# FFN gate/up pieces in four batches of eight instead of eight batches of four, with the down pieces regrouped between them

## The chip, the cores and the metric

One core of one Trainium2 chip. The time is the device time of one execution in microseconds (us); three runs of the kernel before gave 257.48, 257.58 and 261.14, so the median is 257.58 us. A profile is one further execution, recorded instruction by instruction.

## The reference, cut to what matters

```
g   = sigmoid((x * gate_w).sum(-1))                  # a gate per token, 2048 tokens of 1024
q, k, v = split(x @ wqkv); pq, pk = phi(q), phi(k)   # phi: x+1 above 0, else exp(x), plus 1e-6
kv  = sum over tokens of pk^T v, z = sum of pk       # linear attention, 32 heads of 32
a   = (pq kv / (pq z + 1e-6)) @ wo
i   = argmax(x @ w_r);  s = x[i]                     # ONE token goes through the FFN
y   = ((silu(s @ w_gate) * (s @ w_up)) @ w_down) * sigmoid((x @ w_r)[i])
b   = x, with y added to row i
out = g * a + (1 - g) * b
```

w_gate and w_up are 1024 x 3584, w_down is 3584 x 1024, all bf16. One token uses them, so in the FFN there is little to compute and 22 MB of weights to fetch.

## The kernel before, in words

TensorE is fed in units. A K/V unit (`unit_KV(t, nb)`) is eight matmuls of 128x512 for the 128 tokens of block t and a quarter nb of the K and V columns; a Q unit (`unit_Q`) is eight such matmuls for the queries; `unit_KVACC(t)` is eight short matmuls that add block t to the kv sums. ScalarE and VectorE turn each unit's PSUM tile into phi (`phi_exp`, `phi_evac`) and free it; there are four such tiles. The main loop (L510 to L530) runs over t = 4 to 15: four K/V units, the KVACC of the block before after the second of them, then one or two Q units.

The FFN of the chosen token is hung into this loop in pieces. A gate/up piece (`gate_up`) is one load of 128 rows of w_gate or w_up (L385; 512 KB in the first half of the columns, 384 KB in the second) and four matmuls that use 32 columns of the array each, side by side. Eight pieces add up in one PSUM tile; after the eighth piece of gate comes silu (exp on ScalarE; add, reciprocal and product on VectorE), after the eighth of up the product h. A half is therefore 16 pieces, first gate, then up. `h_transpose` (called by `ffn_flush` at the next FFN step) turns h into columns. A down piece (`down_rows`) is one load of two groups of 128 rows of w_down (L433, 512 KB) and two VectorE operations on 128x1024 (L441, L443) that add into `yacc`. There are 14: the first eight need the first half of h only.

All pieces share one ring of nine SBUF tiles (`ffw`, FFN_DEPTH = 9). `ffn_pieces` (L447) gives the order in which they are fetched and used. `ffn_prefetch` (L458) keeps nine in flight: a load goes to the queue of SP as soon as a piece has been used, and its tile must have been released. The first nine loads stand behind the fetch of the chosen row (L358); after the last piece comes a copy of x to the scratch tensor xp (L464), into which the finished row is written later (L504).

GU_AFTER (L34) says after which unit a batch of gate/up pieces is used: (7, 1) is after the K/V unit (7, 1), (7, "end") after the Q units of t = 7. DOWN_STEPS (L35) gives the VectorE steps of the down pieces, from t = 9 on. From the router on, `strict[0]` is False: the wrapper of L77 then writes no program order for TensorE, VectorE and ScalarE, and the framework's scheduler orders each engine's instructions at compile time, by its own idea of when operands are there and which instruction stands earlier in the program. In the trace TensorE's order is the program's nearly everywhere. [...]

Of the kernel before, what the change touches and what calls it, by code (L numbers as in the profile page):

```python
# [30 lines left out]
LN1EPS = math.log1p(EPS)  # L31
N_WARM = 6
Q_PER_T = {4: 2, 5: 1, 6: 1, 7: 2, 8: 1, 9: 1, 10: 2, 11: 1, 12: 1, 13: 2, 14: 1, 15: 0}
GU_AFTER = {(6, "end"), (7, 1), (7, "end"), (8, 1), (8, "end"), (9, "end"), (10, "end"), (11, "end")}  # L34
DOWN_STEPS = {9: (1, 1, 1, 1), 10: (1, 1, 1, 1), 11: (1, 1, 1, 1), 12: (1, 1, 1, 1, 1), 13: (1, 1, 1, 1), 14: (1, 1, 1, 1), 15: (1, 1, 1)}  # L35
FFN_DEPTH = 9
NORM_PER_T = [2, 0, 0, 3, 3, 3, 3, 3, 3, 3, 3, 3, 3, 3, 3, 3]
# [3 lines left out]
def kernel(  # L41
# [180 lines left out]
    def unit_KV(t, nb):  # L222
        kv_open(t)
        ps = ps_work.tile([P, 512], F32, tag="w")
        kv_mm(ps, t, nb, 0, KC)
        kv_evac(ps, t, nb)

    def unit_KVACC(t):
        for g in range(NG):
            pe.matmul(kv_slot(g), lhsT=pk_t[t][:, g * P : (g + 1) * P], rhs=vt_t[t][:, g, :],  # L230
                             start=False, stop=False, skip_group_check=True)
        del pk_t[t], vt_t[t]

    def unit_Q(g, j):
        ps = ps_work.tile([P, 512], F32, tag="w")
        for c in range(KC):
            pe.matmul(ps[:], lhsT=wq[:, c, g * P : (g + 1) * P], rhs=xT[:, c, 512 * j : 512 * j + 512],
                             start=(c == 0), stop=(c == KC - 1))
        phi_evac(ps[:], pq_all[:, g, 512 * j : 512 * j + 512])
# [104 lines left out]
    def router_part1():  # L344
        strict[0] = True
        dve.tensor_reduce(out=rmax[:], in_=c4[:, :, 0], axis=mybir.AxisListType.X, op=ALU.max)
        pen = rt.tile([1, 4], F32)
        strict[0] = False
        dve.tensor_scalar(pen[:], c4[:, :, 0], rmax[0:1, 0:1], None, op0=ALU.is_equal)
        dve.tensor_scalar(pen[:], pen[:], -1.0e6, 1.0e6, op0=ALU.mult, op1=ALU.add)  # L350
        dve.tensor_tensor(pen[:], pen[:], c4[:, :, 1], op=ALU.add)
        idx_f = rt.tile([1, 1], F32)
        dve.tensor_reduce(out=idx_f[:], in_=pen[:], axis=mybir.AxisListType.X, op=ALU.min)
        idx_i = rt.tile([1, 1], I32)
        dve.tensor_copy(idx_i[:], idx_f[:])
        nonlocal_idx[0] = idx_val = nc.values_load(idx_i[0:1, 0:1], engines=(mybir.EngineType.Pool,), min_val=0, max_val=S - 1)
        nc.gpsimd.dma_start(out=xsel_row[:], in_=x2d[bass.ds(idx_val, 1), :])
        xsel_ld[0] = nc.gpsimd.dma_start(out=xsel4[0:128:32, :], in_=x2d[bass.ds(idx_val, 1), :].rearrange("o (j n) -> (o j) n", j=4))  # L358
        dve.tensor_copy(rmax_bf[:], rmax[:])

    def router_part2():
        xs_ps = ps_ffn.tile([P, KC + 1], F32, tag="f")
        for c in range(KC):
            pe.matmul(xs_ps[:, c : c + 1], lhsT=xsel_row[0:1, c * P : (c + 1) * P], rhs=one_bf[0:1, 0:1],
                             start=True, stop=True)
        pe.matmul(xs_ps[:, KC : KC + 1], lhsT=ones_row[0:1, :], rhs=rmax_bf[0:1, 0:1], start=True, stop=True)
        dve.tensor_copy(xs_pad[:, :, 0], xs_ps[:, 0:KC])
        act.activation(sig[:], xs_ps[:, KC : KC + 1], ACTF.Exp, scale=-1.0)
        dve.tensor_scalar_add(sig[:], sig[:], 1.0)
        dve.reciprocal(sig[:], sig[:])  # L370
# [55 lines left out]
    def down_rows():  # L426
        wdv = B_w_down.rearrange("(k p) n -> p k n", p=P)
        pairs = [(7 * j + b, 1) for b in (0, 2) for j in range(4)]
        pairs += [(7 * j + 4, 1) for j in range(4)] + [(6, 7), (20, 7)]
        for i2, (k0, dk) in enumerate(pairs):  # L430
            def load(k0=k0, dk=dk):
                wt = ffw.tile([P, 2048], BF, tag="ffw")
                ld = nc.sync.dma_start(out=wt[:].rearrange("p (k n) -> p k n", k=2), in_=wdv[:, k0 : k0 + dk + 1 : dk, :])  # L433
                tc.add_manual_dep(ld.ins, ffn_state["last_ld"].ins.name, NOSYNC, reason="queue order")
                ffn_state["last_ld"] = ld
                return wt

            def compute(wt, kk, i2=i2, k0=k0, dk=dk):
                w, h1 = wt[:, 1024 * kk : 1024 * kk + 1024], hcol[:, k0 + dk * kk : k0 + dk * kk + 1]
                if i2 == 0 and kk == 0:  # L440
                    dve.tensor_scalar(yacc[:], w, h1, None, op0=ALU.mult)  # L441
                else:
                    dve.scalar_tensor_tensor(yacc[:], w, h1, yacc[:], op0=ALU.mult, op1=ALU.add)  # L443

            yield load, compute

    def ffn_pieces():  # L447
        gu, dn = gate_up(1), down_rows()
        yield from gate_up(0)
        for _ in range(4):  # L450
            yield from islice(gu, 4)
            yield from islice(dn, 2)
        yield from dn

    pieces = ffn_pieces()
    inflight = deque()

    def ffn_prefetch():  # L458
        while len(inflight) < FFN_DEPTH:
            nxt = next(pieces, None)  # L460
            if nxt is None:
                if not ffn_state.get("copied"):
                    ffn_state["copied"] = True
                    cp = nc.sync.dma_start(out=xp[:], in_=x2d)  # L464
                    tc.add_manual_dep(cp.ins, ffn_state["last_ld"].ins.name, NOSYNC, reason="queue order")
                    ffn_state["last_ld"] = cp
                    gate_logits()
                return
            inflight.append((nxt[0](), nxt[1]))

    def ffn_flush():
        pend = ffn_state.pop("pending", None)
        if pend is not None:
            pend()

    def ffn_step(n):
        for _ in range(n):
            ffn_flush()
            wt, comp = inflight.popleft()
            comp(wt)  # L480
            ffn_prefetch()
# [3 lines left out]
    def down_step(n):  # L485
        for _ in range(n):
            ffn_flush()
            if down["cur"] is None:
                down["cur"] = inflight.popleft()
            wt, comp = down["cur"]  # L490
            comp(wt, down["n"] % 2)
            if down["n"] % 2:
                down["cur"] = None
                ffn_prefetch()
            down["n"] += 1
# [14 lines left out]
    for t in range(4, NT):  # L510
        for nb in range(4):
            unit_KV(t, nb)
            if nb == 1 and t > 4:
                unit_KVACC(t - 1)
            if (t, nb) in GU_AFTER:
                ffn_step(4)
            steps = DOWN_STEPS.get(t, ())
            if nb < len(steps):
                down_step(steps[nb])
        for i in range(Q_PER_T[t]):  # L520
            unit_Q(*q_units.popleft())
            if 4 + i < len(steps):
                down_step(steps[4 + i])
            if t == 4 and i == 0:
                router_part1()
                ffn_prefetch()
        if t == 5:
            router_part2()
        if (t, "end") in GU_AFTER:
            ffn_step(4)  # L530
    unit_Q(*q_units.popleft())
    unit_KVACC(NT - 1)
    down_finish()
# [4 lines left out]
    for i in range(3):  # L538
        n = 3 if i < 2 else 2
# [3 lines left out]
    for i in range(3):  # L543
        n = 3 if i < 2 else 2
# [135 lines left out]
```

## Time and profile before

| what | value |
|---|---|
| median of three runs | 257.58 us |
| the profiled execution: its time | 257.94 us |
| its span, first to last instruction | 256.4 us |
| mean granted TensorE clock | 0.998 |
| TensorE busy | 249.9 us, 97% of the span |
| VectorE, ScalarE, GpSimd busy | 145.7, 126.9, 47.0 us |
| matmuls of a gate/up batch, first half / second half | 16 in 1.05 us / 16 in 0.83 us |
| one step into `yacc` | 1281 ns, 27 of them, and a first of 753 ns |
| first weight load issued; copy to xp issued | 57.44 us; 125.62 us |

A line of a timeline gives start, duration, engine, line, operation, tile written <- tiles read, and count. Nearly all compute instructions carry L77, because a wrapper there records them; they are told apart by their tiles: `ps<-wkv,xT` is K/V, `ps<-xT,wq` is Q, `ps<-wt,xs_pad` is gate/up, `yacc<-wt` is down. The engine SPq with `wt<-in_B_w_gate_dram` and its like is the issue of a weight load; the data lands later, and "to landing" says how much later.

### The profile page before, as it was taken

How to read it: one execution, taken by the hardware profiler on the slowest of the kernel's cores; microseconds unless marked ns; L12 is line 12 of the kernel's file. 1: busy time of each engine (PE TensorE's matmuls, PEld its weight loads, DVE VectorE, ACT ScalarE, POOL GpSimd, SP SyncE). 2: the span in 40 equal slices, each digit the busy share in tenths (PEclk: the TensorE clock that was granted, in tenths of full speed). 3: DMA queues.
4: the chain of work that ended last, by engine and by line, in shares of the span. 5: the costliest groups of instructions: out<-in, count | busy, mean ns of one | idle time of the engine just before them, and what ended most of it. 6: DMA issues, size and time to landing. Idle time of an engine off the chain costs nothing.

```text
span 256.4 us, 3781 instructions
## 1 busy us (share of the span) xinstructions
PE 249.9 (97%) x1400; PEld 116.6 (45%) x1426; DVE 145.7 (57%) x238; ACT 126.9 (49%) x202; POOL 47.0 (18%) x99
## 2 busy tenths in 40 slices
PE   8999999999999999999999999999999999999994
PEld 3444454454444444444444444444444444444443
DVE  0055024324155368996899723575986779954443
ACT  2195324545354444654445646466899732352210
POOL 6000001010000000000000000012997029960000
PEclk9999999999999999999999999999999999999999
DMA  6999992007999999879898100077000473454222
GB/s 189 307 330 189 238 315 76 0 3 239 354 348 348 340 336 344 255 227 328 270 438 276 4 0 0 4 234 237 1 3 0 121 233 119 164 179 149 84 82 82
DMA packets 47257, 47.71 MB, mean 186 GB/s; under 512 B 18364, under 2 KB 35140, under 8 KB 47176
## 3 DMA queue, kind: packets, MB, share of 16 engines
q1 hardware_dynamic: 46952, 47.34, 60.3%
q8 instruction: 11, 0.18, 0.3%
q0 software_dynamic: 256, 0.14, 0.2%
q14 instruction: 6, 0.05, 0.1%
q10 hardware_dynamic: 32, 0.00, 0.0%
HBM read 39.34 MB, written 8.40 MB: 186 GB/s over the span
## 4 chain that ended last, share of the span: by engine, by line
PE 95%; DMA 2%; issue 1%; SPq 1%; DVE 0%
PE ps L77 87%; PE kvacc L77 3%; PE first L77 2%; DMA wkv<-in_A_wqkv_dram 2%; PE dps L77 1%; PE rps L77 1%; SPq L77 1%; PE yps L77 0%; DVE ot L77 0%; PE pt L77 0%; PE xs_ps L77 0%; PE hps L77 0%; PE wps L77 0%
## 5 line engine op out<-in xcount | busy, mean ns | idle before, releaser
L77 PE MATMUL ps<-wkv,xT 128*128 128x512 bf16 x467 | 107.2, 380 | 0.6
L77 PEld LDWEIGHTS <-xT 128*128 128x128 bf16 x512 | 48.7, 98 | 58.9 <-issue 4.2
L77 PE MATMUL ps<-xT,wq 128*128 128x512 bf16 x249 | 58.0, 380 | 0.3
L77 ACT ACTIVATE u<-ps 128x512 f32<-128x512 f32 x60 | 35.8, 596 | 40.5 <-PE ps L77 37.2
L77 PE MATMUL ps<-m_sb,pq_all 128*128 128x512 bf16 (+1 forms) x259 | 55.2, 373 | 0.4 <-issue 0.2
L77 ACT ACTIVATE e<-u 128x512 f32<-128x512 f32 x64 | 40.4, 632 | 1.7
L77 PEld LDWEIGHTS <-pq_all 128*128 128x128 bf16 x264 | 25.7, 98 | 29.9 <-issue 0.4
L77 PEld LDWEIGHTS <-wq 128*128 128x128 bf16 x256 | 24.8, 98 | 30.4 <-issue 0.8
L594 POOL TENSOR_TENSOR pq_all<-pq_all,rb 128x512 bf16<-128x512 bf16 x32 | 36.0, 1160 | 8.7 <-DVE rb L77 8.7
L77 DVE SCALAR_TENSOR_TENSOR yacc<-wt,hcol,yacc 128x1024 f32<-128x1024 bf16 x27 | 34.6, 1281 | 3.7 <-DMA wt<-in_B_w_down_dram 3.1
L77 ACT CAST vt<-ps 128x512 bf16<-128x512 f32 x32 | 18.8, 588 | 34.5 <-PE ps L77 34.5
L77 DVE SCALAR_TENSOR_TENSOR pq_all<-ps,e 128x512 bf16<-128x512 f32 x32 | 21.6, 684 | 21.3 <-ACT e L77 21.3
L77 DVE SCALAR_TENSOR_TENSOR ot<-ps,gate,xg 128x512 bf16<-128x512 f32 (+1 forms) x33 | 23.7, 725 | 16.5 <-PE ps L77 15.0
L77 ACT ACTIVATE xg<-xt,omg 128x1024 f32<-128x1024 bf16 x16 | 18.2, 1147 | 25.9 <-DVE ot L77 25.9
L77 DVE SCALAR_TENSOR_TENSOR pk<-ps,e 128x512 bf16<-128x512 f32 x28 | 19.2, 687 | 20.1 <-ACT e L77 20.1
L77 DVE STREAM_SHUFFLE rb<-rdp 128x512 f32<-128x512 f32 x32 | 22.4, 736 | 0.0
L209 POOL MEMSET vt<- 128x8 bf16 x16 | 1.9, 137 | 105.7 <-PE kvacc L77 105.7
L77 PEld LDWEIGHTS <-pk 128*128 128x128 bf16 x128 | 8.5, 98 | 3.3 <-issue 0.4
L77 PE MATMUL kvacc<-vt,pk 128*128 128x129 bf16 x128 | 9.7, 221 | 0.1
L77 ACT CAST m_sb<-ps 128x512 bf16<-128x512 f32 x16 | 9.3, 583 | 0.0
L77 PE MATMUL first<-wkv,xT 128*128 128x512 bf16 x31 | 7.8, 396 | 0.6 <-DMA wkv<-in_A_wqkv_dram 0.6
L77 DVE RECIPROCAL rd<-dn 128x512 f32<-128x512 f32 x2 | 6.7, 3353 | 2.1 <-ACT dn L77 2.1
(96 smaller groups left out, 76.4 us busy)
## 6 DMA issues: line engine op xcount, KB each, us to landing
wt<-in_B_w_down_dram SPq DMA_DIRECT2D x14, 512.0 KB, 5.7
wt<-in_B_w_gate_dram SPq DMA_DIRECT2D x8, 512.0 KB, 7.0
wt<-in_B_w_up_dram SPq DMA_DIRECT2D x8, 512.0 KB, 8.8
xt<-xp SPq DMA_DIRECT2D x16, 256.0 KB, 2.7
out_dram<-ot SPq DMA_DIRECT2D x15, 256.0 KB, 2.0
wt<-in_B_w_gate_dram SPq DMA_DIRECT2D x8, 384.0 KB, 7.6
wt<-in_B_w_up_dram SPq DMA_DIRECT2D x8, 384.0 KB, 7.1
wkv<-in_A_wqkv_dram SPq DMA_DIRECT2D x8, 256.0 KB, 5.0
```

What stands on the lines that cost most here:

```text
L77: inst = fn(*a, **k)
L209: nc.gpsimd.memset(vt_t[t][:, :, 128:129], 1.0)
L594: nc.gpsimd.tensor_tensor(sl, sl, rb[:], op=ALU.mult)
```

## The change

Three things are edited. Half of the places in GU_AFTER go, and at each of the four that stay eight pieces are used instead of four: a whole gate or up accumulation of one half. The first place stays (6, "end"), so pieces 5 to 8 are used there and no longer at (7, 1). And the order of the second half's pieces changes: before, it was four gate/up, two down, four times over; now it is two down, eight gate, four down, eight up, and the other eight down. FFN_DEPTH, DOWN_STEPS and all the rest stay.

```diff
-GU_AFTER = {(6, "end"), (7, 1), (7, "end"), (8, 1), (8, "end"), (9, "end"), (10, "end"), (11, "end")}
+GU_AFTER = {(6, "end"), (8, 1), (9, "end"), (11, "end")}
...
         yield from gate_up(0)
-        for _ in range(4):
-            yield from islice(gu, 4)
-            yield from islice(dn, 2)
+        for n in (2, 4):
+            yield from islice(dn, n)
+            yield from islice(gu, 8)
         yield from dn
...
             if (t, nb) in GU_AFTER:
-                ffn_step(4)
+                ffn_step(8)
...
         if (t, "end") in GU_AFTER:
-            ffn_step(4)
+            ffn_step(8)
```

## The prediction

> **What bounds the kernel now.** I read, in this order: the page (busy times, chain of waits), the timeline of TensorE around the gate/up batches, the timeline of SP with the landings of the loads, and the stages as windows. From the page:
>
> ```profile
> PE 249.9 (97%) x1400; PEld 116.6 (45%) x1426; DVE 145.7 (57%) x238; ACT 126.9 (49%) x202; POOL 47.0 (18%) x99
> ...
> PE 95%; DMA 2%; issue 1%; SPq 1%; DVE 0%
> ```
>
> TensorE carries 95% of the chain that ended last. From the first weight load to the end it is never idle for more than 0.2 us, so a microsecond that is added to its stream, as work or as waiting, is a microsecond of the kernel; and one saved is saved. TensorE's timeline at the first two batches:
>
> ```profile
> 65.80 1.89 PE L77 MATMUL ps<-xT,wq 128*128 128x512 bf16 x8
> 67.62 1.05 PE L77 MATMUL ps<-wt,xs_pad 128*32 128x512 bf16 x16
> 68.60 3.63 PE L77 MATMUL ps<-wkv,xT 128*128 128x512 bf16 x15
> 72.06 0.64 PE L77 MATMUL kvacc<-vt,pk 128*128 128x129 bf16 x8
> 72.63 1.17 PE L77 MATMUL ps<-wt,xs_pad 128*32 128x512 bf16 x16
> ```
>
> The batch at 67.62 takes 1.05 us, its twin at 72.63 takes 1.17: the second already waited about 0.1 us for a load. Which one? SP's timeline, then the answers on the tile wt for the issues at 60.8 and 62.1 and for the one at 65.95, then the stages as windows (length, busy time of PE, PEld, DVE, ACT, POOL, granted clock, DMA share, GB/s):
>
> ```profile
> 57.44 8.47 SPq L385 DMA_DIRECT2D wt<-in_B_w_gate_dram  x8
> 65.95 1.41 SPq L385 DMA_DIRECT2D wt<-in_B_w_up_dram  x1
> ```
>
> ```profile
> L385 SPq DMA_DIRECT2D wt<-in_B_w_gate_dram x2: 1170/1843/2516, 60.8 to 62.1; - x2
> ...
> DMA to landing us min/median/max: 9.8/9.8/9.8
> ```
>
> ```profile
> L385 SPq DMA_DIRECT2D wt<-in_B_w_up_dram x1: 1410/1410/1410, 66.0 to 66.0; - x1
> ...
> DMA to landing us min/median/max: 8.9/8.9/8.9
> ```
>
> ```profile
> 69.10:73.40 4.30, 4.30 (x36) 2.09 (x36) 1.30 (x2) 2.33 (x4) 0.13 (x1) 1.00 1.09 348
> ```
>
> The seventh gate load lands at 62.05 + 9.8 = 71.85, the ninth load of all (up) at 65.95 + 8.9 = 74.86. The loads are one stream of 512 KB at 348 GB/s, 1.5 us each, so the eighth gate load, between the two, lands at about 73.35. That is when the batch at 72.63 could finish: its last piece starts at 73.39. The pieces are used about as fast as they arrive. Counting back by 1.5 us: the fourth piece landed at 67.3, the fifth lands at 68.85, the sixth at 70.35.
>
> [...] Matmuls of 512 columns start 0.2155 us apart within a kind; from the last Q matmul (67.311) to the first gate/up one (67.620) it is 0.309, from the last gate/up group (68.278) to the next K/V matmul (68.599) it is 0.321, and the one after it comes 0.01 late: 0.093 + 0.105 + 0.01 = 0.21 us per batch. In the second half (384 columns) it is 0.309 and 0.267 - 0.163, the same. [...]
>
> **The change, part by part.**
>
> 1. Four batches fewer. The matmuls are the same 128; four switches in and out go: 4 x 0.21 = -0.84 us. The 0.1 us wait of the batch at 72.63 goes as a place of its own: -0.10.
>
> 2. The first batch wants eight loads where four are there. It stays at 67.62. With eight pieces its last group would start at 67.62 + 7 x 0.2155 = 69.13, but its load lands at 73.35, so it starts at about 73.39 as before. [...] behind the waiting matmul are the K/V units of t = 7, which hid this wait before (4.0 us, 68.60 to 72.63). Cost: 73.39 - 69.13 = +4.26 us. The stall comes in pieces of about 1.3 us, a group of matmuls whenever a load lands. ScalarE, VectorE and their PSUM tiles only run dry; nothing of theirs is late afterwards beyond what TensorE is.
>
> 3. Does the stream of loads catch up later? Nothing can be won back: TensorE has no other wait in this stretch that the delay could fill. Nor does the next batch wait. Pieces 1 to 4 free their tiles as before, 5 to 8 sooner, so the stream runs on at its rate, piece 16 lands near 85.4, and batch two comes near 88.4 (73.72 where K/V resumes, plus the 15.06 us of units between, less two switches of 0.2).
>
> 4. The new order of the loads. Ten loads (the second down piece on) now wait for batch two instead of following single pieces. The queue runs empty from about 87 to 89. Each later batch has one piece that depends on a down piece:
>  - The eighth gate piece of the second half takes the tile of the first down piece, so it is issued after two yacc steps. Those follow h_transpose, which follows K/V (9, 0): from the end of batch two 4 x 1.73 + 0.3 + 0.3 + (0.75 + 0.68 + 1.28) = 10.2 us, plus 3.3 to 3.5 us to land on an empty queue (a down load issued at 114.86 took 3.5): 13.7. Batch three wants this piece after eight units, a KVACC and the transpose, 14.7, and seven pieces of 0.163, so 15.8: margin 2.1 us.
>  - The eighth up piece takes the tile of the fifth down piece: two loads of slack less, but six units later; margin about 4 us.
>  - 16 yacc steps are left after batch four: 16 x 1.285 + 8 phis of 0.68 = 26 us from about 128, ending near 154.5; the sum over yacc is wanted at 163.3 + 3.3: margin 12.
>  - The copy to xp, last on SP's queue: eight down loads from 127 (12 us) and the copy's own 12 us (129.9 to 141.93 before) end near 151.5; row and gates need it at about 167. GpSimd's queue is moved past nothing: its row write waits for VectorE's brow as before.
>  I cost part 4 at nothing; if the first margin were used up, each microsecond past it would be one on TensorE.
>
> Sum against the profiled execution: 257.94 + 4.26 - 0.84 - 0.10 = 261.26. The median of the runs lies 0.36 below that execution, so I give 260.9 us, +1.3%. A measurement of this kernel tells about 2% (5.15 us) from no change.
>
> **The unknown in it: the order that the scheduler chooses.** Program order is not forced here, and the scheduler does move a batch behind K/V work when it thinks its operands late: at 92.02 two K/V matmuls stand before the batch of (8, "end"), whose PSUM tile was not yet free. If it thinks the loads late at (6, "end"), it puts K/V matmuls of t = 7 between the pieces. Two things speak against that. Batch (7, 1) stands in program order although its last load was late on the chip. And in these lines of VectorE and of ScalarE
>
> ```profile
> 118.47 1.28 DVE L77 SCALAR_TENSOR_TENSOR yacc<-wt,hcol,yacc 128x1024 f32<-128x1024 bf16 x1 [2.45 <-DMA wt<-in_B_w_down_dram]
> 119.67 0.68 DVE L77 SCALAR_TENSOR_TENSOR pk<-ps,e 128x512 bf16<-128x512 f32 x1
> ```
>
> ```profile
> 117.11 0.63 ACT L77 ACTIVATE e<-u 128x512 f32<-128x512 f32 x1
> ```
>
> a yacc step stands ahead of a phi that was ready at 117.74 and comes earlier in the program; the step's load landed at 118.37. So the scheduler had it landing at least 0.6 us sooner than it did: it is an optimist about loads. From both sides: all of the wait filled, -0.94 us; none, +3.32. I take none.
>
> **Rivals.**
>
> - A, as above: the pieces in program order, the clock stays. 260.9 us. Chance 0.58.
> - B, half filled: the scheduler sees the last pieces 1 to 2 us late and puts five to nine K/V matmuls ahead of them. Each 0.2155 us moved up saves that, each extra switch costs 0.2: the gain is about 1.4, 259.5 us. Chance 0.16.
> - C, the other side, not slower: its idea of the loads is as slow as the chip's, and the K/V units (6, "end") to (7, 1) fill the wait wholly. Then only the switches count: 257.58 - 0.94 = 256.6, or up to 257.6 with pieces split. It decides if the eighth load is expected about 4 us after the last Q matmul; from 3.3 us of filling on there is no loss. For it: the matmuls exist and depend on nothing. Against: the optimism shown. Chance 0.07.
> - D, the clock: for 5 us TensorE works 15% of the time. [...] Against: no gap is over 1.4 us. From 1.8 us on it makes the kernel over 2% slower. Chance 0.12.
> - E, a second stall: the margin of 2.1 us in part 4 fails, or VectorE stands behind a down load so long that the four PSUM tiles fill. For it: VectorE did stand 2.45 us at 118.47. Against: four tiles are some 5 us of units. 1 to 3 us more: 262 to 264. Chance 0.07.
>
> **The numbers.** Predicted is A, 260.9. The range 258.3 to 263.5 holds A, B, the lower halves of D and E; left out are C and the tails, about 0.15. Over 2% faster (under 252.4) no case reaches: 0.01. Over 2% slower (over 262.7): most of D and about half of E, 0.12. The rest, 0.87, is within 2%, nearly all of it on the slow side.
>
> **What would show it.** Right: one line of gate/up matmuls at about 67.6 that lasts some 6 us, with waits for DMA wt inside; K/V resuming near 73.7; four batches near 67.6, 88.4, 104.9 and 126; after that TensorE as dense as before and shifted by 3.3. Clock 1.00 in the window from 73 to 80 excludes D. K/V matmuls between gate/up ones near 68 to 73 show B or C. A wait on w_gate near 105 shows E. If K/V resumes near 69.4, the loads were earlier than I think and the reading of the landings is wrong.

## The result, and the profile after

The kernel after takes 265.76 us (median of four runs, 264.72 to 267.13), the kernel before 257.54 (four runs): ratio 1.029 over all runs, 95% interval 1.021 to 1.038 (the two medians alone give 1.032). It is slower, in the forecast direction, but by two and a half times what was forecast (+8.2 us instead of +3.3) and above the range's end of 263.5. The profiled execution took 265.26 us with a span of 263.7, 7.3 more than before; mean clock 0.986 instead of 0.998.

The page of the kernel after, its first section, TensorE's clock in 40 slices and the chain that ended last:

```profile
PE 251.4 (95%) x1400; PEld 117.4 (45%) x1426; DVE 145.3 (55%) x238; ACT 126.9 (48%) x202; POOL 47.0 (18%) x99
...
PEclk9999999999959999999999999999999999999999
...
PE 84%; DMA 8%; SPq 3%; DVE 3%; issue 1%; ACT 0%; DVEq 0%; POOLq 0%
```

TensorE's part of the chain fell from 95% to 84%; loads, the queue that issues them and VectorE now stand in it. And in one slice (72 to 79 us) the clock was granted at about half. TensorE's timeline there:

```profile
67.89 1.05 PE L77 MATMUL ps<-wt,xs_pad 128*32 128x512 bf16 x16
69.20 0.40 PE L77 MATMUL ps<-wt,xs_pad 128*32 128x512 bf16 x4 [0.27 <-DMA wt<-in_B_w_gate_dram]
70.70 0.40 PE L77 MATMUL ps<-wt,xs_pad 128*32 128x512 bf16 x4 [1.10 <-DMA wt<-in_B_w_gate_dram]
72.21 0.62 PE L77 MATMUL ps<-wt,xs_pad 128*32 128x512 bf16 x4 [1.10 <-DMA wt<-in_B_w_gate_dram]
73.72 0.62 PE L77 MATMUL ps<-wt,xs_pad 128*32 128x512 bf16 x4 [0.90 <-DMA wt<-in_B_w_gate_dram]
74.27 0.61 PE L77 MATMUL ps<-wkv,xT 128*128 128x512 bf16 x1
75.10 5.06 PE L77 MATMUL ps<-wkv,xT 128*128 128x512 bf16 x14 [0.22 <-issue]
80.00 0.64 PE L77 MATMUL kvacc<-vt,pk 128*128 128x129 bf16 x8
```

Pieces 5 to 8 come one by one, 1.5 us apart, each when its load lands. The K/V matmuls of t = 7, which need no FFN weight, stand behind them and start only at 74.27: TensorE kept its order through the whole wait. The records then get longer, 0.62 instead of 0.40 for the same four matmuls. The stages as windows (length, busy PE, PEld, DVE, ACT, POOL, granted clock, DMA share, GB/s):

```profile
68.65:72.06 3.41, 1.09 (x16) 0.20 (x8) 0.69 (x1) 0.60 (x1) 0.00 (x0) 1.00 1.09 348
72.06:78.89 6.83, 5.57 (x18) 1.86 (x19) 3.78 (x2) 1.55 (x3) 0.00 (x0) 0.50 1.09 348
78.89:82.30 3.41, 3.41 (x23) 1.84 (x22) 1.98 (x3) 1.50 (x3) 0.13 (x1) 1.00 1.09 347
```

After 3.41 us with TensorE busy for 1.09 of them the clock is 0.50, for 6.83 us, two such windows. Later there is one more wait, shown by TensorE's timeline, by the chain of waits around it and by VectorE's timeline:

```profile
130.60 1.90 PE L77 MATMUL ps<-wkv,xT 128*128 128x512 bf16 x8
133.56 0.23 PE L77 MATMUL hps<-sel,h_bf 128*128 128x4 bf16 x3 [1.06 <-DVE h_bf L77]
```

```profile
125.00 1.20 DVE yacc L77
...
126.22 3.51 DMA wt<-in_B_w_down_dram
...
129.83 1.30 DVE yacc L77
...
131.15 1.28 DVE yacc L77
132.43 0.60 DVE pq_all L77
133.03 0.48 DVE h_bf L77
...
133.56 0.23 PE hps L77 x3
```

```profile
129.83 2.61 DVE L77 SCALAR_TENSOR_TENSOR yacc<-wt,hcol,yacc 128x1024 f32<-128x1024 bf16 x2 [3.03 <-DMA wt<-in_B_w_down_dram]
132.35 0.68 DVE L77 SCALAR_TENSOR_TENSOR pq_all<-ps,e 128x512 bf16<-128x512 f32 x1
132.95 0.55 DVE L77 TENSOR_TENSOR h_bf<-ps,sg 128x384 bf16<-128x384 f32 x1
```

The last step of the sixth down piece (125.00) frees a ring tile; only then is the seventh down load issued (126.22), which takes 3.51 us to land. VectorE has two of that piece's steps ahead of the product h of the second half and stands idle 3.03 us until the load lands; the transpose of h on TensorE (`hps`) waits for h. In the program it is the other way round: by the end of t = 11 only twelve steps into `yacc` have been written, then comes h, then the seventh piece. In the trace fourteen stand ahead of h (sixteen in before): the scheduler moved two of them forward.

The sum, from the two traces. The last group of the first batch starts 73.72 - 67.89 = 5.83 us after the first instead of 7 x 0.2155 = 1.51: +4.32. From there to the KVACC it is 6.28 us, at full clock 16 x 0.2155 + 0.33 = 3.78: +2.50. From K/V (12, 0) to the next KVACC it is 4.77 us, before 3.54: +1.23. Four switches and the old small wait, as priced in the prediction: -0.94. Together +7.1, and the first batch began 0.27 us later: +7.4, measured +7.3.

### The profile page after: what moved, and what is told of

Same layout as the page of the kernel before. It is cut to its first block, busy times and chain, and to the rows that moved or that the text cites. A ratio compares the mean times of both kernels' runs of the same rounds, so it can differ in the third digit from the quotient of the medians.

```text
span 263.7 us, 3784 instructions
## 1 busy us (share of the span) xinstructions
PE 251.4 (95%) x1400; PEld 117.4 (45%) x1426; DVE 145.3 (55%) x238; ACT 126.9 (48%) x202; POOL 47.0 (18%) x99
## 4 chain that ended last, share of the span: by engine, by line
PE 84%; DMA 8%; SPq 3%; DVE 3%; issue 1%; ACT 0%; DVEq 0%; POOLq 0%
PE ps L77 77%; DMA wt<-in_B_w_gate_dram 3%; SPq L385 3%; PE kvacc L77 3%; PE first L77 2%; DMA wkv<-in_A_wqkv_dram 2%; DVE yacc L77 2%; DMA wt<-in_B_w_down_dram 1%; DMA xsel<-in_A_x_dram 1%; PE dps L77 1%; PE rps L77 1%; SPq L77 1%; DVE pq_all L77 0%; ACT u L77 0%; DVE pk L77 0%
## 5 line engine op out<-in xcount | busy, mean ns | idle before, releaser
L77 PE MATMUL ps<-wkv,xT 128*128 128x512 bf16 x467 | 109.4, 384 | 0.9 <-issue 0.2
L77 PEld LDWEIGHTS <-xT 128*128 128x128 bf16 x512 | 49.5, 99 | 60.7 <-issue 6.3
L77 DVE SCALAR_TENSOR_TENSOR pk<-ps,e 128x512 bf16<-128x512 f32 x28 | 19.2, 687 | 15.8 <-ACT e L77 15.8
L77 PE MATMUL ps<-wt,xs_pad 128*32 128x512 bf16 (+1 forms) x128 | 8.0, 368 | 3.4 <-DMA wt<-in_B_w_gate_dram 3.4
```

The costliest lines, as they stand in the source:

```text
L77: inst = fn(*a, **k)
```

## The experiments

The theory had these three terms: the wait for loads, the clock after it, and the second wait. Rivals: the clock falls for another reason; the second wait is only a consequence of the delay; VectorE simply has too much to do there. Ratios are against the kernel before on the same chip (its median was 257.9 to 258.4).

**One part alone: the first batch.** The kernel before, with its order of the pieces; only the first two batches are joined.

```diff
-GU_AFTER = {(6, "end"), (7, 1), (7, "end"), (8, 1), (8, "end"), (9, "end"), (10, "end"), (11, "end")}
+GU_AFTER = {(6, "end"): 8, (7, "end"): 4, (8, 1): 4, (8, "end"): 4, (9, "end"): 4, (10, "end"): 4, (11, "end"): 4}
...
-                ffn_step(4)
+                ffn_step(GU_AFTER[(t, nb)])
...
-            ffn_step(4)
+            ffn_step(GU_AFTER[(t, "end")])
```

> Before with one part of the change alone: the first two batches (pieces 1 to 8) are used together after (6, end); all other batches of four and the old order of the pieces stay. Three-term theory (4.3 us of waiting for loads 5 to 8, then 2.5 us because the clock is granted at half for two windows of 3.4 us, then 1.2 us of a second wait that comes from the new order of the pieces): the first two terms are here, the third is not: 257.5 + 4.3 - 0.2 - 0.1 + 2.5 = 264.0 us, mean clock 0.986, no wait before the second transpose of h. Rival 'the clock falls for another reason than the wait': 261.5 us and 0.998. Rival 'the second wait follows from the delay, not from the order': 265.2 us with a wait near 133 us.

Measured: 263.96 us, ratio 1.020 (1.017 to 1.023), clock 0.986 to 0.993. Both first terms are here, +5.15 us of waiting and +1.73 by the clock in the profile (the eighth load landed late, at about 74.2); no transpose waits:

```profile
67.64:71.05 3.41, 1.40 (x21) 0.51 (x21) 0.69 (x1) 1.23 (x2) 0.00 (x0) 1.00 1.09 348
71.05:77.88 6.83, 4.87 (x20) 1.49 (x20) 2.31 (x2) 0.60 (x1) 0.00 (x0) 0.50 1.09 349
```

**The change without its first part.** The kernel after, with the number of pieces beside each place.

```diff
+GU_AFTER = {(6, "end"): 4, (7, 1): 4, (8, 1): 8, (9, "end"): 8, (11, "end"): 8}
```

> The change without its first part: batches of four after (6, end) and (7, 1) as before, then eights after (8, 1), (9, end) and (11, end) with the new order of the pieces. Three-term theory: three batches fewer, -0.6 us, the second wait of TensorE before the second transpose of h stays, +1.2: 258.1 us, clock 0.998. Rival 'batches of eight narrow matmul groups lower the clock by themselves': 260 us or more with a half-rate stretch. Rival 'the second wait follows from the delay': 256.9 us, no wait.

Measured: 259.55 us, ratio 1.004 (1.002 to 1.006), clock 0.998 or more in thirteen of fourteen runs and 0.993 in one. Eights alone don't lower the clock, and the second wait is there without the delay of the first batch, so it belongs to the new order:

```profile
128.11 0.23 PE L77 MATMUL hps<-sel,h_bf 128*128 128x4 bf16 x3 [1.28 <-DVE h_bf L77]
```

The expected ratio was 1.002. In this execution the eighth gate load landed about a microsecond later than in the profile of before, and the batch at (7, 1), still of four, waited 0.83 us for it.

**Work put into the wait.** The kernel after, with matmuls on constants before pieces 6, 7 and 8.

```diff
+                        if half == 0 and wi == 0 and c > 4:
+                            fps = ps_work.tile([P, 512], F32, tag="w")
+                            for _ in range(4):
+                                pe.matmul(fps[:], lhsT=warm_w, rhs=warm_x, start=True, stop=True)
```

> The kernel after with filler: before pieces 6, 7 and 8 of the first batch four matmuls of 128x512 on constants go to a PSUM tile that nobody reads, so that TensorE works while it would wait for the loads. Twelve matmuls are 2.6 us, with the switches 3.7, all within the 4.3 us of waiting. Three-term theory: the wait stays, the clock stays at full rate: 265.8 - 2.5 = 263.3 us, clock 0.998. Rival 'the clock falls for another reason than the low activity in the wait': 265.8 us, clock 0.986.

Measured: 262.19 us, ratio 1.014 (1.011 to 1.017), clock 1.00 in all four runs. TensorE's timeline:

```profile
68.71 1.05 PE L77 MATMUL fps<-const-bfloat16-1.0 128*128 128x512 bf16 x4
69.89 0.40 PE L77 MATMUL ps<-wt,xs_pad 128*32 128x512 bf16 x4
...
72.90 0.40 PE L77 MATMUL ps<-wt,xs_pad 128*32 128x512 bf16 x4
73.23 3.63 PE L77 MATMUL ps<-wkv,xT 128*128 128x512 bf16 x16
```

The last piece is nearly as late as ever (5.5 us after the first, 5.8 in after), but K/V resumes at full speed: 3.63 us for sixteen matmuls. With twelve more matmuls the kernel is faster than after (1.014 against 1.029). The wait itself still costs; the fall of the clock came from the quiet in it. The time is 1.1 us less than expected; the second wait was 0.61 us here, a little over half of what it was in after.

**The first batch two units later.**

```diff
+GU_AFTER = {(7, 1), (8, 1), (9, "end"), (11, "end")}
```

> The kernel after with the first batch of eight moved from (6, end) to (7, 1), two K/V units and a KVACC later (4.0 us). Three-term theory: the eighth load is there within 0.2 us of its use, so the first term shrinks to 0.2 and the clock stays at full rate; four batches fewer, -0.8, -0.1; the second wait stays, +1.2: 258.0 us, clock 0.998. Rival 'the second wait follows from the delay': 256.8 us.

Measured: 259.75 us, ratio 1.0045 (1.003 to 1.006), clock 0.998 or more in all twenty runs. The stall shrank from 4.3 us to one wait of 1.02 us (0.2 was expected: here too the eighth load came later, at about 74.4), and the second wait was 1.19. The two together are more than the switches saved.

**The kernel after again, beside three more.** The first is unchanged.

> The kernel after once more, unchanged, beside the next three on the same chip. Three-term theory: 264 to 267 us, clock 0.986 with a stretch of 6.8 us at half rate, wait of TensorE of about 1 us before the second transpose of h. Nothing here tells the theories apart; it is the measure for the others.

Measured: 264.37 us, ratio 1.026 (1.022 to 1.029). The mean clock was 0.993 or 0.994 in three of the four runs, and 0.987 in one; the profile shows one half-rate window (72.89 to 76.30, 3.41 us; clock 0.994), not two. So the price of the clock is not the same in every run. The second wait was 1.64 us.

```diff
-FFN_DEPTH = 9
+FFN_DEPTH = 10
```

> The kernel after with ten tiles in the ring instead of nine. Theory of the third term: the sixth to last group of down loads (the seventh down piece) is issued only when the fifth-last step has freed its tile, lands 3.5 us later, and VectorE stands in front of it with h behind; with a tenth tile it is issued one release earlier, VectorE does not wait 3 us, h comes in time: 1.0 to 1.2 us less than the kernel after on this chip, no wait of the hps matmuls over 0.2 us; first wait and clock as in after. Rival 'VectorE has simply too many steps there': no change, and the wait before hps stays.

Measured: 264.32 us, ratio 1.020 (1.013 to 1.027). As times the two don't differ; the clock differed from run to run (0.987, 0.987, 0.998, 0.993 here), by more than the term in question. Taken behind the clock's stretch, from the KVACC of block 6 to the sum over yacc, it is 170.09 - 80.14 = 89.95 us against 90.62 in after and 91.20 in its repetition, and the wait before the transpose is 0.37 us. The seventh down load landed at 125.49, some four microseconds sooner, and most of the wait went, not all: VectorE now ran four steps of the seventh and eighth down piece ahead of h, the last until 131.90.

With two filler matmuls instead of four:

> As the run with four filler matmuls before pieces 6, 7 and 8, but two: TensorE computes about 43% of the time between the loads. If a half-busy window keeps the clock: 2.5 us less than the kernel after on this chip and clock 0.998; if not: as the kernel after, 0.986.

Measured: 262.28 us, ratio 1.016 (1.012 to 1.021), clock 1.00. And with one:

> The same with one filler matmul before each of the three pieces: about 29% of the time between the loads. Three-term theory expects the clock to fall here, as with 14% without filler: as the kernel after, 0.986. If 29% is enough: 2.5 us less and 0.998.

Measured: 263.92 us, ratio 1.025 (1.019 to 1.031). Neither expectation held in full: the clock was 1.00 in two of the four runs and 0.987 and 0.986 in the other two. The profile is one of the first two; in it the batch began late, at 69.48, and its pieces span only 4.6 us.

**Six pieces, then two.**

```diff
+GU_AFTER = {(6, "end"): 6, (7, 1): 2, (8, 1): 8, (9, "end"): 8, (11, "end"): 8}
```

> The kernel after with six pieces used after (6, end) and two after (7, 1), then eights as in after. Three-term theory: the wait for loads 5 and 6 is about 2.2 us (the sixth lands near 70.4 to 71), the two last cost nothing; [...] the second wait stays: 257.9 + 2.2 - 0.6 + 1.2 = 260.7 us and clock 0.998. If windows that are only partly quiet also halve the clock: 1.7 to 2.5 us more and a half-rate stretch of 3.4 or 6.8 us.

Measured: 260.87 us, ratio 1.012 (1.007 to 1.017). In the profile one wait of 1.11 us for a load is left, 1.4 us of lateness in all where 2.2 was expected; the second wait was 1.58. The clock was 1.00 in two runs and 0.993 in two; those two have no trace, but the profile of the repetition above, with its one half-rate window, has 0.994. So this stall seems to have halved the clock too, in two runs of four.

**h ahead of the late steps.** One ordering dependency on VectorE, nothing else.

```diff
+                    step = dve.scalar_tensor_tensor(yacc[:], w, h1, yacc[:], op0=ALU.mult, op1=ALU.add)
+                    if i2 == 6 and kk == 0:
+                        tc.add_manual_dep(step.ins, ffn_state["h"].ins.name, NOSYNC, reason="h of the second half first")
```

> The kernel after with one dependency more, for the order alone: the first step of the seventh down piece stands behind the product h of the second half in VectorE's order. Theory of the third term (VectorE's order puts steps whose load is late ahead of h): the wait of the hps matmuls goes wholly, 1.1 to 1.6 us less than the kernel after, first wait and clock as in after: near 263.3 us. Rival 'VectorE has too many steps there': the wait goes but comes back at a later unit, no gain.

Measured: 263.03 us, ratio 1.018 (1.013 to 1.023). On VectorE h now stands ahead of the two steps, and the transpose follows its unit at once:

```profile
130.39 1.90 PE L77 MATMUL ps<-wkv,xT 128*128 128x512 bf16 x8
132.12 0.22 PE L77 MATMUL hps<-sel,h_bf 128*128 128x4 bf16 x3
```

```profile
130.98 0.55 DVE L77 TENSOR_TENSOR h_bf<-ps,sg 128x384 bf16<-128x384 f32 x1
131.44 2.60 DVE L77 SCALAR_TENSOR_TENSOR yacc<-wt,hcol,yacc 128x1024 f32<-128x1024 bf16 x2
```

From the KVACC of block 6 to the sum over yacc it is 169.18 - 79.78 = 89.40 us, 1.2 less than in after, 1.8 less than in its repetition, so the wait did not come back later: the order was the cause, not the amount of work.

**All three costs taken out.** Places after (7, 2), (8, 2), (9, end) and (11, end), h first, and ten tiles; then the same with nine.

```diff
+GU_AFTER = {(7, 2), (8, 2), (9, "end"), (11, "end")}
+FFN_DEPTH = 10
```

> All three costs removed and the four switches kept saved: batches of eight after (7, 2), (8, 2), (9, end) and (11, end), the order of h before the steps of the seventh down piece, ten tiles in the ring. Three-term theory: no wait at the first batch (the eighth load lands 73.0 to 74.5, its use is near 75), clock 0.998 or more, no wait before hps: before - 0.84 - 0.1 = ratio 0.996. Rival 'there is a fourth cost': ratio 1.000 or more.

> The same with nine tiles in the ring as in before and after. Three-term theory: the stream of loads stands for about 1 us while the first batch is not yet used, the second batch after (8, 2) is late enough to hide it: ratio 0.996 as well. If the ring then is the limit, there is a wait of up to 1 us at the second batch: ratio 1.000.

Measured: with ten tiles 257.39 us, ratio 0.9964 (0.9951 to 0.9976); with nine 257.73, ratio 0.998 (0.9965 to 0.9997). The first is 0.4% faster than before, about what the four switches were worth (-0.94 us is 0.9964; the interval is 0.3 us to either side). In its profile one other wait of TensorE is left, at 110.52, for a PSUM tile whose phi (`pk`) came late on VectorE. This is the stall at the PSUM tiles that rival E named, and it is not in the profile of after (view of the waits: us in total, times, longest):

```profile
PE ps L77 <- DVE pk L77: 0.7, 1, 0.7
```

So a fourth cost can occur; how often it does in the other runs isn't known. The first two batches with ten tiles, and in the second fence the second batch with nine tiles, where the ring let the stream of loads stand while the first batch was not yet used:

```profile
73.47 1.91 PE L77 MATMUL ps<-wt,xs_pad 128*32 128x512 bf16 x32
...
86.25 1.91 PE L77 MATMUL ps<-wt,xs_pad 128*32 128x512 bf16 x32
```

```profile
88.32 0.40 PE L77 MATMUL ps<-wt,xs_pad 128*32 128x512 bf16 x4 [0.88 <-DMA wt<-in_B_w_up_dram]
```

## Why the prediction was wrong

**Right: the first two steps.** The switches (-0.84, -0.10) are, within 0.3 us, what the version with ten tiles and all three costs taken out gained. The wait in step 2 was put at 4.26 us and measured 4.32 in the profile of after; in the four other profiles with the same first batch and no filler it was 4.05 to 5.15, so the mechanism was right and the agreement to a tenth is luck. It came in program order, with the gaps of some 1.1 us that the landings 1.5 us apart leave. The scheduler moved no K/V matmul into it, so rivals B and C are out. The margin of 2.1 us for the eighth gate piece of the second half was 2.1: it landed at 106.78 and was used at 107.73 + 7 x 0.163 = 108.87.

**Wrong, first: rival D was given 0.12, with "no gap is over 1.4 us" against it.** I took a fall of the clock to need one long unbroken idle stretch; that was an assumption of mine, and no trace shows it. In after the 3.41 us before the fall (68.65 to 72.06) had two groups of matmuls in them and no gap over 1.1 us, and the clock then stood at 0.50 for 6.83 us. The term that A put at nothing is +2.50 us in the profiled execution and 1.6 to 2.8 in the four others. The run with four fillers shows the cause: nearly the same wait (5.5 us from the first piece to the last, 5.8 in after) without the quiet, and the clock stayed at 1.00.

**Wrong, second: step 4, "I cost part 4 at nothing".** I went through the pieces whose tile comes from a down piece, but only those of the gate/up batches, and took the later down loads for a stream that has 12 us. The first of them, the seventh down piece, has none: its tile is that of the sixth, whose last step ends at 126.2, three microseconds before batch four, and two of its steps stand on VectorE ahead of h, which TensorE wants 1.7 us after batch four. My "16 yacc steps are left after batch four" took the program's order for VectorE's; in the trace fourteen were left. I had asked what the scheduler would do on TensorE only. I had the evidence in hand. The 2.45 us at 118.47 in the profile before is this very queueing, and I used it only to argue about the scheduler and, in rival E, about the PSUM tiles. Measured: +1.23 us in after, and waits of 0.6 to 1.6 us in the seven other profiles with nine tiles, the new order and no dependency for h. In the old order VectorE's wait for a down load lay four steps and 6 us before h and harmed nothing.

**Wrong, third: the cases were laid side by side.** A, D and E exclude one another in my list, but D follows from A's wait and E is independent of it. Their sum, 260.9 + 2.5 + 1.2 = 264.6, is near the measured 265.8; the 1.2 us that is left is within the spread of the four runs (264.7 to 267.1), and no run explains it.

What stays open is small. The landing of the eighth load varied by about 2 us between profiles (72.2 to 74.4; 15.8 to 17.3 us after the issue of the first weight load), for which I have no cause; batches placed at its edge pay for it. The kernel after gave 265.8 and, repeated, 264.4; the mean clock (0.985 or 0.986 in all four runs there, 0.993 or 0.994 in three of four here) says two half-rate windows against one, in the profiles +2.50 us against +1.59, which would be most of it.

## What to carry to other kernels

When work is gathered into one batch, the last operand of the batch must be there at its start; look up the landing of that one load, and count what the separate places used to hide. In these profiles a wait on TensorE of 4.05 to 5.15 us had a second price, the clock (1.6 to 2.8 us), though single matmuls ran inside it: look for such a fall in the trace, and add its price to the wait instead of listing it as an unlikely alternative. And in a ring, follow the first load after each batch, too: ask who frees its tile, and what stands behind its user on that engine; where a scheduler sets the order, read it in the trace and not in the program.

## What the runs showed of the hardware

What the clock did after partly busy stretches can be read off these profiles. The half-rate stretch lasted 6.83 us in after and 3.41 in its repetition, so I took the 3.41 us before each fall and counted TensorE as busy for the columns that it streamed, not for the whole length of the records: 512 columns take the 0.2155 us that K/V matmuls are apart, 0.426 in the half-rate stretch of after, and four matmuls side by side count once. In after, the window 68.65 to 72.06 holds the end of the first batch (0.12 us) and two pieces (0.23 each), so it is 0.17 busy. In the five profiles in which the clock fell, the window before the fall was 0.13 (the repetition), 0.17 (after), 0.18 (h first), 0.19 (ten tiles) and 0.31 busy (first batch alone), with one profile behind each figure. Three profiles in which it did not fall have no window of 3.41 us in the stall, wherever it is laid, that is less than 0.44 (two fillers), 0.53 (six pieces) and 0.66 busy (four fillers). With one filler the quietest place is 0.31 busy in the profile, where the clock stayed at 1.00; it fell in two of that kernel's four runs. What decides between these was not shown. To come back took more: after half-rate windows that were 0.32 (first batch alone) and 0.49 busy (after) the clock stayed at half, after 0.94 (the repetition), 0.96 (first batch alone) and 1.00 (after) it was full again. The fall came at a different time from run to run (71.05 us in the first batch alone, 72.06 in after, 72.89 in the repetition), and nearly the same stall cost two windows of 3.41 us, one, or, in one run with ten tiles (clock 0.998), none.
